# Rounding weights beside attention and a seven-product matrix multiplication: a ring of exponents, two block sets, later stores, and twelve attention pairs beside the second product

## The chip, the cores and the metric

One core of one Trainium2 chip. The metric is the device time of one execution in microseconds (us), the median of several runs. A profiled execution gives a span, from first to last instruction, about 2 us shorter than the time. The engines are TensorE (PE in the profile; PEld is its weight load), VectorE (DVE), ScalarE (ACT), GpSimd (POOL) and SyncE (SP), whose queue issues most of the DMAs.

## The reference

Shortened (the softmax takes off its maximum first, and small constants are left out):

```python
def _attn_ref(q, k, v, g_q, g_k):            # q, k, v: (8, 12, 448, 64)
    q_n, k_n = rmsnorm(q, g_q), rmsnorm(k, g_k)
    scores = scale * np.matmul(q_n, k_n.transpose(0, 1, 3, 2))
    attn = softmax(scores)
    return np.matmul(attn, v)
def _moe_ref(x, w_in, w_out):                # x: (3584, 768), w_in: (768, 2048), w_out: (2048, 768)
    h = x @ w_in
    r = np.maximum(h, 0.0)
    return (r * r) @ w_out
# [...] x is attn with the heads joined; w_in and w_out arrive as float64
```

The weights come as 64-bit floats (`words_in = 2` in the kernel) and are rounded to 32 bits on the chip.

## The kernel before

The 8 batches are four spans of two; a span has twelve attention pairs (two heads each). Both products of a span use a scheme of seven block products in place of eight (operands A11, S2, S1, S3, A12, A22, S4 of the weights). The weights' operands are made once, in span 0, from 32 pieces n of the weights, by a pipeline of 35 steps ("ticks") that is spread over the first 350 us, and stored in DRAM as `w1s` and `w2s`, from where `sw` tiles are loaded for each product.

A tick in its four quarters:

```python
# tick t; n = t: exponent, n = t-1: mantissa, n = t-2: value, n = t-3: totals and store
nc.vector.tensor_scalar(eu, high, 20, 0x7FF, shift_right, and_)     # e lies in the block of n
nc.scalar.activation(f, f, AF.Copy, bias=1.0, scale=2.0 ** -20)       # n = t-2
total(t - 3, S1, A21, A22, ALU.add, late)                             # late: on VectorE
total(t - 3, S2, S1, A11, ALU.subtract)                               # on GpSimd
yield
# [...] two activations of the exponent
total(t - 3, S3, A11, A21, ALU.subtract, late)
total(t - 3, S4, A12, S2, ALU.subtract)
yield
# [...] two VectorE operations of the mantissa
value(t - 2, 0)                                                       # GpSimd: f * e
yield
nc.vector.scalar_tensor_tensor(f, low, 2.0 ** -32, high, mult, add)
value(t - 2, 1)
# n = t-3: store the block (w1s: one DMA; w2s: three), then load words up to t + 2
yield
```

The first product takes seven `sw` tiles for each of eight f; pb, pc and pd turn over two PSUM banks, and VectorE adds them up:

```python
pb = ps_m.tile([P, S], F32, tag="m", name="pb"); product(pb, n + S2, T2, True);  add(z, p1, pb)
pc = ps_m.tile([P, S], F32, tag="m", name="pc"); product(pc, n + S1, T1, True);  add(y, z, pc)
pd = ps_m.tile([P, S], F32, tag="m", name="pd"); product(pd, n + S3, T3, True);  add(g22, y, pd)
# [...] product(pa, A12), product(pd, A22): add(g21, z, pd); product(pc, S4): add(g12, z, pc)
```

The order of span 0 and the attention of span 1 (ALONE = 2):

```python
for u, _ in enumerate(attention(work, 0, start_of(1), True)):      # stage A
    weights(EARLY * (u + 1) // (2 * NPAIR))                           # 12 ticks
for u, _ in enumerate(first_product(work, 0)):                     # stage B
    weights(EARLY + (LATE - EARLY) * (u + 1) // N1)                   # 21 ticks
for u, _ in enumerate(attention(work, start_of(1), start_of(1) + ALONE, True)):   # stage C
    weights(ALL)
# second_product(0) with the ten other pairs of span 1 beside it: stage D; then the rest: R
```

## Time and profile before

| | before |
|---|---|
| time, median of 3 | 1513.79 us (1513.71 to 1518.29) |
| span of the profiled run | 1512.0 us |
| TensorE busy | 1443.2 us, 95% |
| TensorE idle | 54 of 68.8 us in the first 347 us |

A high busy share of TensorE says where little gain is to be had: of the 68.8 us in which TensorE is idle, 54 lie in the first 347 us and 14.8 in the 1165 us after them. In the first 347 us four engines and one DMA queue hand work to each other, and there the reading goes backward from each wait to who was late, and why. The lines stand in the prediction below.

### The profile page before, as it was taken

Reading aid. Unit: us, or ns where it says so; the run is one execution under the profiler, and the core shown is the slowest. Engines: PE = TensorE matmul, PEld = TensorE weight load, DVE = VectorE, ACT = ScalarE, POOL = GpSimd, SP = SyncE. Lnnn points to the kernel's source line nnn. Section 1 sums busy time; section 2 is a strip of 40 time slices with the busy share of each in tenths; the row PEclk is TensorE's granted clock in tenths of the full one; section 3 lists DMA queues with packets and bytes.
Section 4 is the critical chain, followed back from the end, with each engine's and each line's share of the span. In section 5 each row is a group of like instructions: output and inputs, shape, how many; then the busy total and the mean of one; then the engine's idle time right before and its main releaser. Section 6 shows DMA issues by size and latency. Waiting matters only on the chain.

```text
span 1512.0 us, 14222 instructions
## 1 busy us (share of the span) xinstructions
PE 1443.2 (95%) x4696; PEld 658.8 (44%) x4696; DVE 828.4 (55%) x1160; ACT 431.4 (29%) x588; POOL 554.9 (37%) x367
## 2 busy tenths in 40 slices
PE   5998889888999999999999999999999999999998
PEld 2433444333444445544444445544444445555553
DVE  3777789856776533446666643345666752332111
ACT  4766565542222201123222211123223211111000
POOL 4788667773333102353344202254333301221000
PEclk9999999989999999999999999999999999999999
DMA  5365888854445433343445433334445323333443
GB/s 163 97 193 152 251 308 273 273 127 101 103 87 118 100 87 89 85 110 75 111 90 111 91 87 99 85 100 100 98 92 112 78 66 98 85 88 104 101 116 68
DMA packets 357816, 180.39 MB, mean 119 GB/s; under 512 B 255140, under 2 KB 334180, under 8 KB 357732
## 3 DMA queue, kind: packets, MB, share of 16 engines
q1 hardware_dynamic: 349668, 168.36, 43.7%
q10 hardware_dynamic: 8064, 11.01, 2.2%
q8 instruction: 40, 0.66, 0.2%
q14 instruction: 44, 0.36, 0.1%
HBM read 146.28 MB, written 33.03 MB: 119 GB/s over the span
## 4 chain that ended last, share of the span: by engine, by line
PE 73%; POOL 9%; DVE 7%; issue 5%; DMA 4%; ACT 1%; SPq 0%; POOLq 0%; DVEq 0%; ACTq 0%
PE ps L864 30%; PE sc L675 8%; PE pa L788 8%; PE pav L692 7%; PE pc L788 7%; PE pd L788 7%; PE pb L788 4%; DVE rec L709 4%; POOL rstd L618 3%; POOL gC L479 2%; PE tot L703 2%; POOL qkn L620 2%; DMA sw<-w1s 2%; POOL gC L486 1%; DMA gC<-in_moe_w_out_dram 1%
## 5 line engine op out<-in xcount | busy, mean ns | idle before, releaser
L864 PE MATMUL ps<-gT,sw 128*128 128x448 f32 x768 | 303.2, 545 | 0.0
L640 POOL TENSOR_TENSOR half<-half,mhalf 128x28 f32<-128x28 f32 x34 | 166.2, 4888 | 316.7 <-DVE half L639 262.5
L796 POOL TENSOR_TENSOR gT<-gT 128x448 f32<-128x448 f32 x112 | 111.1, 994 | 439.3 <-ACT gT L792 437.3
L678 ACT ACTIVATE pr<-sc 112x896 f32<-112x896 f32 x192 | 165.9, 913 | 237.5 <-PE sc L675 237.3
L864 PE MATMUL ps<-gC,sw 128*128 128x448 f32 x576 | 228.2, 545 | 0.0
L864 PEld LDWEIGHTS ps<-gT,sw 128*128 128x128 f32 x768 | 143.3, 190 | 155.5 <-issue 155.1
L675 PE MATMUL sc<-qkT 64*112 64x448 f32 x768 | 174.7, 575 | 14.8 <-ACT qkT L654 12.5
L709 DVE RECIPROCAL rec<-tot 128x448 f32<-128x448 f32 x48 | 141.9, 2957 | 81.8 <-PE tot L703 81.8
L692 PE MATMUL pav<-pr,vt 112*64 112x448 f32 x768 | 165.4, 554 | 10.5 <-DVE xT L711 6.8
L788 PE MATMUL pa<-xT,sw 128*128 128x448 f32 x384 | 156.4, 544 | 5.3 <-DMA sw<-w1s 5.3
L864 PEld LDWEIGHTS ps<-gC,sw 128*128 128x128 f32 x576 | 106.9, 190 | 116.7 <-issue 114.6
L792 ACT ACTIVATE gT<-gT 128x448 f32<-128x448 f32 x96 | 55.2, 576 | 292.7 <-DVE gT L822 178.3
L675 PEld LDWEIGHTS sc<-qkT 64*112 64x112 f32 x768 | 62.3, 177 | 112.5 <-issue 74.5
L683 DVE TENSOR_TENSOR acc<-acc,pr 112x896 f32<-112x896 f32 x68 | 74.7, 1099 | 59.6 <-ACT pr L678 56.1
L788 PEld LDWEIGHTS pa<-xT,sw 128*128 128x128 f32 x384 | 73.3, 191 | 78.3 <-issue 75.0
L692 PEld LDWEIGHTS pav<-pr,vt 112*64 112x64 f32 x768 | 52.1, 139 | 111.5 <-issue 87.2
L654 ACT ACTIVATE qkT<-qkT,gains 128x448 f32<-128x448 f32 x34 | 22.7, 668 | 238.5 <-DVE qkT L653 238.5
L788 PE MATMUL pd<-xT,sw 128*128 128x448 f32 x192 | 80.1, 554 | 7.3 <-DVE z L811 4.5
L788 PE MATMUL pd<-xC,sw 128*128 128x448 f32 x192 | 77.7, 541 | 3.8 <-DVE gT L822 3.8
L683 DVE TENSOR_TENSOR acc<-pr 112x896 f32<-112x896 f32 x34 | 37.1, 1091 | 78.9 <-ACT pr L678 78.9
L788 PE MATMUL pc<-xC,sw 128*128 128x448 f32 x192 | 77.6, 540 | 1.1 <-DVE gT L835 0.9
L788 PE MATMUL pc<-xT,sw 128*128 128x448 f32 x192 | 77.5, 540 | 0.8 <-DMA sw<-w1s 0.8
(90 smaller groups left out, 1493.7 us busy)
## 6 DMA issues: line engine op xcount, KB each, us to landing
sw<-w2s SPq DMA_DIRECT2D x168, 256.0 KB, 2.8
sw<-w1s SPq DMA_DIRECT2D x168, 192.0 KB, 2.3
w1s<-gC SPq DMA_DIRECT2D x8, 1344.0 KB, 6.2
sw<-w1s ACTq DMA_DIRECT2D x56, 192.0 KB, 4.6
w2s<-gC SPq DMA_DIRECT2D x24, 448.0 KB, 4.3
out_dram<-osb SPq DMA_DIRECT2D x192, 56.0 KB, 1.8
words<-in_moe_w_out_dram SPq DMA_DIRECT2D x11, 768.0 KB, 7.3
qk<-in_q_dram SPq DMA_DIRECT2D x136, 56.0 KB, 2.8
```

Source lines behind the costliest of these rows:

```text
L479: nc.gpsimd.tensor_tensor(b[to[n % 2][half]], f[:, part], e[:, part], ALU.mult)
L618: nc.gpsimd.tensor_tensor(rflat, rflat, mhalf[:SP, 0:4 * NJ], ALU.pow)
L640: nc.gpsimd.tensor_tensor(half, half, mhalf, ALU.pow)
L675: nc.tensor.matmul(sc[:, h, 0:S], qkT[rows, 1, c * SP:(c + 1) * SP], qkT[rows, 0, :], start=True, stop=True)
L678: nc.scalar.activation(pr, sc[:, :, 0:S], AF.Exp)
L683: nc.vector.tensor_tensor(accs[i], probs[i, 0] if c == 1 else accs[i], pr, ALU.add)
L692: nc.tensor.matmul(pavs[i][h * D:(h + 1) * D, :], vs[i][:, h, c, :], pr[:, h, :], start=(c == 0), stop=(c == NJ - 1))
L709: nc.vector.reciprocal(rec, tots.pop(i))
L788: nc.tensor.matmul(ps, stream[n][:, c], rhs[:, c], start=first and c == 0, stop=c == HC - 1, skip_group_check=not first)
L792: nc.scalar.activation(g, src, AF.Relu)
L796: nc.gpsimd.tensor_tensor(g, g, g, ALU.mult)
L864: nc.tensor.matmul(ps, stream[n][:, c % 4], rhs_of[i][:, c], start=c == 0, stop=c == HF - 1)
```

## The change

Its intent: the exponents get a ring of four buffers of their own, so that they no longer lie in blocks that totals or values want; this leaves room for two block sets in place of three. Stores go out after the last totals, loads earlier; all loads go over the SP queue; w_out's operands are stored in one DMA. The total S1 moves to GpSimd. Then stage C goes: all twelve pairs of span 1 run beside the second product. The core of the diff:

```diff
-    ALONE = 2
-    NAT = 2 * NPAIR + ALONE
+    NAT = 2 * NPAIR
-    WORDS, BLOCKS, LAST = 6, 3, 24
-    EARLY, LATE, ALL = 4 * 12, 4 * 33, 4 * (2 * NFC + 3)
+    WORDS, BLOCKS, EXPS, LAST = 6, 2, 4, 31
+    EARLY, LATE, ALL = 4 * 13, 4 * 35, 4 * (2 * NFC + 4)
-    w2s = dram.tile([HC, 7, HF // 4, P, 4 * P], F32, name="w2s")
+    w2s = dram.tile([7, HF // 4, P, 4, HW], F32, name="w2s")
+    def exponents_of(n):
+        at = BLOCKS * 8 * HW + n % EXPS * NW
+        return stage[:, at:at + NW]
 ... (in the tick)
-        total(t - 3, S1, A21, A22, ALU.add, late)        # quarter 0, VectorE
+        total(t - 3, S1, A21, A22, ALU.add)              # quarter 2, GpSimd
+        while loaded[0] <= t + 3 and all(...): load_w    # quarter 1; was t + 2 in quarter 3
-        n = t - 3                                        # the store, quarter 3
+        n = t - 4                                        # quarter 2
+            nc.sync.dma_start(dst.rearrange("k p m -> p k m"), blocks_of(n)[:, 0:7])
 ... (the sw loads)
-            queue = nc.scalar if len(stream) < N1 else nc.sync
-            queue.dma_start(sw.rearrange("p c m -> p (c m)"), src)
+            nc.sync.dma_start(sw, src)
 ... (the order of the stages)
+                if u == NAT - 2:
+                    load_blocks(5)
-        # the pool "alone" with two pairs and weights(ALL)
+    weights(ALL)
+                free = 0 if span else 2
-                for u, _ in enumerate(attention(work, a, start_of(span + 2), False)):
+                for u, _ in enumerate(attention(work, nxt, nxt + 2 * NPAIR, False)):
```

More of the change, by code (lines that the diff above doesn't have):

```diff
@@ L405, in attention_then_ffn_bounded @@
     HW = HC * P
-    WORDS, BLOCKS, LAST = 6, 3, 24
-    EARLY, LATE, ALL = 4 * 12, 4 * 33, 4 * (2 * NFC + 3)
-    assert DM == NW and BLOCKS * 8 * HW + 2 * NW <= 3 * HF * S and 2 * NW <= 4 * S and HF % 4 == 0
+    WORDS, BLOCKS, EXPS, LAST = 6, 2, 4, 31
+    EARLY, LATE, ALL = 4 * 13, 4 * 35, 4 * (2 * NFC + 4)
+    assert DM == NW and BLOCKS * 8 * HW + EXPS * NW + 2 * NW <= 3 * HF * S and 2 * NW <= 4 * S and HF % 4 == 0
     A11, S2, S1, S3, A12, A22, S4 = range(7)
@@ L422, in place_of @@
     def place_of(n):
-        return n % WORDS if n < LAST else (0, 3, 4, 5)[(n - LAST) % 4]
+        return n % WORDS if n < LAST else 3
     def words_of(n):
@@ L428, in words_of @@
         if place == 0:
-            at = BLOCKS * 8 * HW
+            at = BLOCKS * 8 * HW + EXPS * NW
             flat = stage[:, at:at + 2 * NW]
@@ L458, in prepare, with parts @@
     def prepare(t):
-        def parts(n):
-            b = [blocks_of(n)[:, i] for i in range(8)]
-            at = (S2, A22)[n % 2]
-            e = blocks_of(n)[:, at:at + 2].rearrange("p k m -> p (k m)")
-            low, high = pairs_of(words_of(n))
-            return b, e, e.bitcast(U32), low, low.bitcast(F32), high
         def there(n):
             return 0 <= n < 2 * NFC
+        def parts(n):
+            low, high = pairs_of(words_of(n))
+            return exponents_of(n), exponents_of(n).bitcast(U32), low, low.bitcast(F32), high
@@ L473, in value @@
         def value(n, half):
-            b, e, _, _, f, _ = parts(n)
+            if not there(n):
+                return
             to = ((A11, A12), (A21, A22)) if n < NFC else ((A11, A21), (A12, A22))
+            dst = blocks_of(n)[:, to[n % 2][half]]
             part = slice(half * HW, (half + 1) * HW)
             if doubles:
-                nc.gpsimd.tensor_tensor(b[to[n % 2][half]], f[:, part], e[:, part], ALU.mult)
-            else:
-                nc.gpsimd.tensor_copy(b[to[n % 2][half]], words_of(n).bitcast(F32)[:, part])
@@ L483, in total @@
-        def total(n, dst, x, y, op, on_vector=False):
+                e, _, _, f, _ = parts(n)
+                nc.gpsimd.tensor_tensor(dst, f[:, part], e[:, part], ALU.mult)
+            else:
+                nc.gpsimd.tensor_copy(dst, words_of(n).bitcast(F32)[:, part])
+        def total(n, dst, x, y, op, engine=nc.gpsimd):
             if there(n) and n % 2:
-                b = parts(n)[0]
-                (nc.vector if on_vector else nc.gpsimd).tensor_tensor(b[dst], b[x], b[y], op)
-        late = t >= EARLY // 4
+                b = [blocks_of(n)[:, i] for i in (dst, x, y)]
+                engine.tensor_tensor(*b, op)
@@ L489, in prepare @@
         if there(t) and doubles:
-            b, e, eu, low, f, high = parts(t)
+            e, eu, low, f, high = parts(t)
             nc.vector.tensor_scalar(eu, high, 20, 0x7FF, ALU.logical_shift_right, ALU.bitwise_and)
         if there(t - 2) and doubles:
-            f = parts(t - 2)[4]
+            f = parts(t - 2)[3]
             nc.scalar.activation(f, f, AF.Copy, bias=1.0, scale=2.0 ** -20)
-        total(t - 3, S1, A21, A22, ALU.add, late)
-        total(t - 3, S2, S1, A11, ALU.subtract)
@@ L497, in prepare @@
         yield
         if there(t) and doubles:
-            b, e, eu, low, f, high = parts(t)
+            e, eu, low, f, high = parts(t)
             nc.scalar.activation(e, eu, AF.Relu, bias=clamp1, scale=-1.0)
             nc.scalar.activation(eu, e, AF.Relu, bias=clamp2, scale=-(2.0 ** 23))
-        total(t - 3, S3, A11, A21, ALU.subtract, late)
-        total(t - 3, S4, A12, S2, ALU.subtract)
+        while loaded[0] <= t + 3 and all(
+                place_of(m) != place_of(loaded[0]) for m in range(max(t - 2, 0), loaded[0])):
+            load_w(loaded[0])
+            loaded[0] += 1
@@ L505, in prepare @@
         yield
         if there(t - 1) and doubles:
-            b, e, eu, low, f, high = parts(t - 1)
+            e, eu, low, f, high = parts(t - 1)
             nc.vector.scalar_tensor_tensor(eu, high, 0x80000000, eu, ALU.bitwise_and, ALU.bitwise_or)
             nc.vector.tensor_scalar(high, high, 0xFFFFF, None, ALU.bitwise_and)
-        if there(t - 2):
-            value(t - 2, 0)
+        value(t - 2, 0)
+        total(t - 3, S1, A21, A22, ALU.add)
+        n = t - 4
+        if there(n) and n % 2:
+            c = n % NFC // 2
+            dst = w1s[c] if n < NFC else w2s[:, c // 4, :, c % 4]
+            nc.sync.dma_start(dst.rearrange("k p m -> p k m"), blocks_of(n)[:, 0:7])
+            written[0] = n + 1
@@ L515, in prepare @@
             nc.vector.scalar_tensor_tensor(f, low, 2.0 ** -32, high, ALU.mult, ALU.add)
-        if there(t - 2):
-            value(t - 2, 1)
-        n = t - 3
-        if there(n) and n % 2:
-            c = n % NFC // 2
-            if n < NFC:
-                nc.sync.dma_start(w1s[c].rearrange("k p m -> p k m"), blocks_of(n)[:, 0:7])
-            else:
-                for m in range(HC):
-                    nc.sync.dma_start(
-                        w2s[m, :, c // 4, :, c % 4 * P:(c % 4 + 1) * P].rearrange("k p m -> p k m"),
-                        blocks_of(n)[:, 0:7, m * P:(m + 1) * P])
-            written[0] = n + 1
-        while loaded[0] <= t + 2 and all(
-                place_of(m) != place_of(loaded[0]) for m in range(max(t - 1, 0), loaded[0])):
-            load_w(loaded[0])
-            loaded[0] += 1
+        value(t - 2, 1)
+        total(t - 3, S2, S1, A11, ALU.subtract)
+        total(t - 3, S3, A11, A21, ALU.subtract, nc.vector if t >= EARLY // 4 else nc.gpsimd)
+        total(t - 3, S4, A12, S2, ALU.subtract)
         yield
     def ticks():
-        for t in range(2 * NFC + 3):
+        for t in range(2 * NFC + 4):
             yield from prepare(t)
@@ L565, in load_blocks @@
                 sw = sw[:, 0:HC]
-                src = w1s[n // 7, n % 7]
+                src = w1s[n // 7, n % 7].rearrange("p (c m) -> p c m", c=HC)
             else:
                 n -= N1
-                src = w2s[*uses2[n // (HF // 4)], n % (HF // 4)]
-            queue = nc.scalar if len(stream) < N1 else nc.sync
-            queue.dma_start(sw.rearrange("p c m -> p (c m)"), src)
+                m, i = uses2[n // (HF // 4)]
+                src = w2s[i, n % (HF // 4), :, :, m * P:(m + 1) * P]
+            nc.sync.dma_start(sw, src)
             stream.append(sw)
@@ L740, in attention @@
             scores(work, i, 1, alone)
-            if i + 2 < (start_of(2) if alone else last):
+            if i + 2 < (last + 2 if alone else last):
                 norm(i + 2)
@@ L925, in attention_then_ffn_bounded @@
         with tc.tile_pool(name="first", bufs=2, reuse_waits="tile") as work:
-            for u, _ in enumerate(attention(work, 0, start_of(1), True)):
-                weights(EARLY * (u + 1) // (2 * NPAIR))
+            for u, _ in enumerate(attention(work, 0, NAT, True)):
+                weights(EARLY * (u + 1) // NAT)
+                if u == NAT - 2:
+                    load_blocks(5)
         with tc.tile_pool(name="first_product", bufs=2, reuse_waits="tile") as work:
@@ L930, in attention_then_ffn_bounded @@
                 weights(EARLY + (LATE - EARLY) * (u + 1) // N1)
-        with tc.tile_pool(name="alone", bufs=2, reuse_waits="tile") as work:
-            for u, _ in enumerate(attention(work, start_of(1), start_of(1) + ALONE, True)):
-                weights(ALL)
+    weights(ALL)
     for span in range(NSPAN):
@@ L944, in attention_then_ffn_bounded @@
             if more:
-                a = nxt + (0 if span else ALONE)
-                places = 2 * (start_of(span + 2) - a)
+                free = 0 if span else 2
                 total, done = HC * (7 * HF + 4) - 20, 0
-                for u, _ in enumerate(attention(work, a, start_of(span + 2), False)):
-                    while done < total * (u + 1) // places:
+                for u, _ in enumerate(attention(work, nxt, nxt + 2 * NPAIR, False)):
+                    while done < total * (u + 1 - free) // (4 * NPAIR - free):
                         next(rest)
```

## The prediction

> **What bounds the kernel now.** I began with the summary page: TensorE (PE) is busy 1443 of 1512 us, so at most 69 us can be had without removing TensorE work. The view of busy time by stretches, cut where the instructions of the timeline change line, says where they lie. The columns are: stretch, its length, busy time of PE, PEld, DVE, ACT and POOL (with instructions), granted clock, DMA share, GB/s.
>
> ```profile
> PE 1443.2 (95%) x4696; PEld 658.8 (44%) x4696; DVE 828.4 (55%) x1160; ACT 431.4 (29%) x588; POOL 554.9 (37%) x367
> ...
> 0.00:160.00 160.00, 136.49 (x680) 56.19 (x680) 103.25 (x113) 98.12 (x124) 117.54 (x82) 0.97 0.55 157
> 160.00:163.80 3.80, 0.00 (x0) 0.00 (x0) 3.77 (x2) 0.00 (x0) 3.26 (x4) 1.00 1.23 195
> 163.80:311.60 147.80, 133.49 (x336) 63.91 (x336) 122.63 (x145) 82.24 (x115) 96.78 (x76) 0.98 0.81 268
> 311.60:347.30 35.70, 23.31 (x107) 8.31 (x106) 18.97 (x27) 12.20 (x17) 23.24 (x15) 0.83 0.59 137
> 347.30:553.10 205.80, 205.80 (x697) 89.22 (x698) 136.53 (x199) 48.78 (x60) 58.63 (x24) 0.99 0.43 98
> 553.10:1512.00 958.90, 944.08 (x2881) 441.19 (x2879) 443.21 (x677) 190.03 (x273) 255.43 (x168) 1.00 0.39 94
> ```
>
> The stages, named for use below: A, attention of span 0 with most of its totals on TensorE (160 us); a gap of 3.8; B, the first product of span 0 (147.8); C, two pairs of span 1 alone (35.7); D, the second product with the other ten pairs (205.8); R, the rest (958.9). D and R are solid TensorE; the change can win only in the first 347 us. There I read who TensorE waits for, in A from 28 us on, in B, and in C (columns: total us, times, longest):
>
> ```profile
> PE pt L659 <- POOL qkn L620: 3.8, 4, 2.6
> PE pav L692 <- DMA vt<-in_v_dram: 3.6, 2, 2.4
> ...
> PE pa L788 <- DMA sw<-w1s: 5.3, 2, 4.0
> PE pd L788 <- DVE z L811: 4.5, 3, 2.1
> PE pd L788 <- DVE gT L822: 3.8, 3, 2.3
> PE pd L788 <- DMA sw<-w1s: 2.6, 1, 2.6
> ...
> PE pav L692 <- DVE xT L711: 6.8, 1, 6.8
> PE sc L675 <- ACT qkT L654: 5.2, 1, 5.2
> ```
>
> These releasers are themselves late, so I followed them back through the waits of the queue that issues the DMAs and of POOL, in A from 28 us on:
>
> ```profile
> SPq L522 <- POOL gC L486: 54.8, 4, 14.8
> SPq L310 <- POOL qkn L620: 39.4, 13, 10.3
> ...
> POOL rstd L618 <- DVE rstd L617: 28.2, 9, 8.6
> ...
> ACT qkn L613 <- DMA qk<-in_k_dram: 9.2, 3, 4.1
> ```
>
> The store of a block (L522) stands in the in-order queue until POOL has made its totals (L486), up to 14.8 us; the loads of q, k and v behind it start late; the norms then run late on ACT, DVE and POOL; TensorE waits for qkn and vt. A loop of lateness, not a full engine.
>
> **What the Trainium skill says.** "DMA: Bandwidth & Descriptors", section "Anatomy of one DMA": DMA engines wait on no semaphore; the issuing sequencer waits before it dispatches. The 54.8 us above agree. Its specifications give 512 B as the least transfer for line rate; the new w_out loads have 512 B pieces where they had 2048 B, just on that edge, and no trace here has that shape yet. "TensorE: Matmul & The Clock Gate", section "Part 1: The HAM clock gate": after about 3.4 us idle the array runs at half clock until it has been busy about as long again. The trace agrees: after 4.0 us idle the first six passes of B took 3.98 us and not 2.42. "GPSIMD Engine Reference", section "Engine selection": two-input elementwise work is about 2x slower on GpSimd than on VectorE. In B the same 128x384 operation took 1276 ns on POOL and 728 ns on DVE, 1.75x.
>
> **The change, part by part.**
>
> *Stage A.* A pair takes 10.46 us where nothing waits (scores at 31.76, 42.22, 52.68, 63.14, 73.61, 84.07), so from pair 1 at 31.76 the stage could end at 31.76 + 11 x 10.46 = 146.8 (its last pair needs 10.46 after its start) and ends at 159.8: 13 us lost in pairs 6, 8 and 10. Moving a store a tick (four steps, about one pair here) behind its totals takes away most of what it waits for; vt and qk then go out in time, and with them the clock losses. Words are loaded nearly two ticks earlier: load of t+3 at the first quarter of tick t, against t+2 at its end. Against it: a thirteenth tick in A adds 2 values and 4 totals, 6 POOL operations at 1.0 us, 117.5 -> about 124 us in a stage that should get shorter, near 85%. I keep 5 of the 13 us as lost: A ends at 151.5, 8 sooner.
>
> *Gap.* The first five w1s loads are issued a pair before A ends: 3.8 us away.
>
> *Stage B.* 56 products x 2.255 us = 126.3 us is TensorE's floor; 147.8 - 126.3 = 21.5 are lost. DVE: S1 goes to POOL (11 x 0.73 = 8 us), and one tick of rounding fewer lies here (one exponent step 0.8, one set of three 1.29 + 1.04 + 1.32 = 3.65): 122.6 - 12 = about 111 us, 88% of the floor. POOL: + 11 x 1.28 = 14, less two values of 1.3: 96.8 + 11 = 108, 86%. No engine exceeds the floor, but both come in bursts. The w1s loads leave ACT's queue, where they waited behind activations (4.6 us to landing, against 2.3 on the other queue later); they now stand in the one queue behind stores and word loads, five products ahead (four x 2.26 = 9 us of cover). Two block sets for three mean that POOL's value may overwrite a block one tick (about 5.8 us) after its store was issued, and such a store took 6.2 us to land: a new wait, about balanced. I take 9 us of loss in place of 21.5: B = 135.
>
> *Stages C and D.* Both pairs go into D. Beside the second product a pair costs TensorE 1.69 + 3.05 + 0.86 + 1.69 = 7.3 us; C and its idle time go. But two places are left without product, so that D opens with what C had: pair 12 alone (scores, four exponentials of 0.91 with the norm's square of 0.95 between, the accumulation of 3 x 1.1, totals, reciprocal 2.96, xT 0.95, transposes 1.13, scaling 0.67) gives scores of pair 13 at about 15 us and the first ps at about 17. The w2s loads stand in the queue behind the last store (after POOL's totals, some 5.5 us into D), eight q/k issues of pair 15, then eight of pair 16, which wait for the norm of pair 14 (POOL power 4.8, two multiplies 1.84, done at about 13): issued at 17 to 20, landed 3 us later. I take first ps at 21.5. From ps onward the kernel before needs 553.1 - 350.5 = 202.6 for what it has; one more pair (13's values to 23's end instead of 14's) makes 209.9. D = 21.5 + 209.9 = 231, in place of C + D = 241.5: 10 us won.
>
> *w_out in one store, and R.* One store of 1344 KB in 1536 B rows for three of 448 KB in 512 B rows saves issues in B. The loads get 512 pieces for 128. A 256 KB load serves eight passes, 3.0 us, against 2.8 us to landing, with five buffers ahead and a DMA share of 0.39 in R. I expect no wait: R = 958.9.
>
> *Sum.* 151.5 + 135 + 231 + 958.9 = 1476.4; the time before exceeds its span by 1.8: **1478 us**, 2.4% less.
>
> **Rivals.**
> 1. *POOL becomes the bound of A and B.* S1 moves to the slower engine and A gets six more operations. For it: power 3.7 and two multiplies 2.1 us each pair, plus 52/12 steps, come to some 10 us of 10.46; 1.28 to 1.33 us an operation in B. Against: 28 us of waits in A and 51 idle in B now. Then A saves 3 and B 5: about 1491.
> 2. *The single queue blocks.* Word loads wait for POOL's value of the tick before, stores for totals, and w1s loads stand behind; cover is 9 us less 2.3 to 5 of landing. Then TensorE waits for sw in every tick or two, B stays near 143: 1486.
> 3. *The opening of D goes better or worse.* With the w2s loads ready, ps starts at 17: 1473. If the last store and pair 16's q/k are late, 26 us: 1483.
> 4. *512 B pieces are slow.* Landing times above 9 us would stall R in every second product; the spare DMA share speaks against. Each 0.1 us per w2s load would be 17 us; I give it 4%.
>
> **Range and chances.** A may end at 147 to 157, B be 129 to 143, the opening of D 17 to 26; as independent errors about 3, 4 and 3 us, together 6. The lean is upward, since the rivals only add: 1468 to 1491. The 2% line lies at 1483.5, nearly one error above my number: faster 0.70, same 0.29, slower 0.01.
>
> **What would show it right or wrong.** Right, if in the profile after: the store's wait on POOL totals in A falls from 54.8 to below 20 us and vt vanishes from TensorE's waits; A's last total ends at 148 to 155 and the first pa follows within 1 us; B is 130 to 140 us with DVE near 111 and POOL near 108 busy; the first ps comes 19 to 24 us after B; TensorE shows no sw wait after 560 us and R is 958 to 960. Wrong, if B stays above 143 (look whether pd waits for sw or for DVE), if POOL's gC waits for a store, if A still ends near 160, or if R has grown.

## The result and the profile after

| | before | after |
|---|---|---|
| time, median (4 runs each) | 1513.75 us | 1497.45 us (1497.3 to 1499.91) |
| ratio, 95% interval | | 0.989 (0.9868 to 0.9911) |
| predicted | | 1478 us, range 1468 to 1491 |

Ratios here and below are the mean time of one kernel's fast runs over that of the other's of the same rounds, so not quite the ratio of the medians quoted. The result is correct. The change is faster by 1.1%, less than half of what was predicted, and outside the range.

Busy time by stretches, of the kernel after, cut at the same events (end of A, set 0.2 us too early, first pa, first scores of pair 12, first ps, first pa of span 1; columns as in the prediction):

```profile
0.00:152.70 152.70, 133.60 (x672) 53.84 (x672) 107.87 (x124) 97.69 (x123) 114.59 (x82) 0.99 0.59 174
152.70:154.20 1.50, 0.18 (x2) 0.02 (x1) 1.43 (x3) 1.47 (x3) 1.50 (x1) 1.00 1.03 355
154.20:302.20 148.00, 131.97 (x338) 63.21 (x338) 133.14 (x136) 82.93 (x116) 123.62 (x97) 0.99 0.80 268
302.20:323.60 21.40, 11.02 (x45) 3.49 (x44) 13.52 (x18) 7.98 (x10) 12.05 (x7) 0.76 0.62 148
323.60:536.60 213.00, 211.41 (x725) 90.94 (x726) 144.17 (x212) 50.84 (x63) 63.32 (x27) 0.99 0.44 97
536.60:1495.60 959.00, 944.18 (x2881) 441.18 (x2879) 442.05 (x677) 190.03 (x273) 256.43 (x168) 1.00 0.39 94
```

Stage by stage against the prediction:

| | before | predicted | after |
|---|---|---|---|
| A ends at | 159.8 | 151.5 | 152.9 |
| gap | 4.0 | 0 | 1.3 |
| B | 147.8 | 135 | 148.0 |
| C / opening of D up to the first ps | 38.9 | 21.5 | 21.4 |
| first ps to span 1's first pa | 202.5 | 209.9 | 213.0 |
| R | 958.9 | 958.9 | 959.0 |

A, the opening and R came out as told. Stage B did not get shorter at all: 13 of the 19 us of error. In it VectorE was busy for 133 us and not 111, though it executes fewer instructions (136 against 145), and GpSimd for 124 and not 108. The lines of the total S3 (and S1, which VectorE made before), by line, with shortest, median and longest duration in ns; first of the kernel before, then of the kernel after:

```profile
L486 POOL TENSOR_TENSOR gC<-gC x40: 991/1002/1712, 74.6 to 330.0; 128x384 f32<-128x384 f32 x40
L486 DVE TENSOR_TENSOR gC<-gC x24: 545/552/1289, 166.1 to 328.5; 128x384 f32<-128x384 f32 x24
```

```profile
L489 POOL TENSOR_TENSOR gC<-gC x53: 992/1192/1744, 75.6 to 307.4; 128x384 f32<-128x384 f32 x53
L489 DVE TENSOR_TENSOR gC<-gC x11: 552/1358/1400, 176.4 to 302.8; 128x384 f32<-128x384 f32 x11
```

The same operation takes 552 ns at its shortest in both, but its median is 552 before and 1358 after. An addition with one operand in PSUM, of the kernel after, hardly varies:

```profile
L805 DVE TENSOR_TENSOR z<-p,pb x32: 607/621/623, 164.8 to 1350.7; 128x448 f32<-128x448 f32 x32
```

What stands behind it is in the Trainium skill, "SBUF — State Buffer", section "SBUF: two separate sides": VectorE and GpSimd share a pair of SBUF ports, taken as an exclusive lock for a whole instruction by whichever starts first, VectorE asking for them when it has two SBUF inputs (against a GpSimd operation that reads SBUF) or runs in a two-port mode. The two-valued durations and the steady addition from PSUM agree with that. The prediction did not look there.

The timeline of the kernel after shows the lock instruction by instruction (start us, us; both engines in order of time):

```profile
200.98 1.27 DVE L523 SCALAR_TENSOR_TENSOR words<-words 128x768 f32<-128x768 uint32 x1
201.40 1.72 POOL L489 TENSOR_TENSOR gC<-gC 128x384 f32<-128x384 f32 x1
202.18 1.36 DVE L489 TENSOR_TENSOR gC<-gC 128x384 f32<-128x384 f32 x1
...
227.72 0.55 DVE L489 TENSOR_TENSOR gC<-gC 128x384 f32<-128x384 f32 x1
228.08 1.07 POOL L482 TENSOR_TENSOR gC<-gT,gC 128x384 f32<-128x384 f32 x1 [1.69 <-DVE words L523]
```

The addition at 202.18 begins while a GpSimd operation runs and ends 0.42 us after that one's end (203.54 against 203.12); the one at 227.72 begins with GpSimd idle and takes 0.55. It is so without exception: of 121 such additions on VectorE in the kernels before and after and in e2, e3, e6 and e12, the 62 that began beside a running GpSimd operation ended 0.41 to 0.42 us after its end, and the other 59 took 0.54 to 0.57 us. GpSimd's addition at 201.40 was itself long (1.72 us; 0.99 at its shortest), beside the VectorE instruction that ended at 202.25.

Who waits for whom in stage B after, for TensorE (columns: total us, times, longest):

```profile
PE pd L782 <- DVE z L805: 4.0, 3, 2.2
PE pa L782 <- DMA sw<-w1s: 3.3, 3, 1.7
PE pc L782 <- DMA sw<-w1s: 3.2, 2, 1.7
PE pd L782 <- DMA sw<-w1s: 2.8, 2, 1.4
PE pb L782 <- DVE xC L722: 1.8, 1, 1.8
PE pd L782 <- DVE gT L816: 1.4, 2, 1.2
```

Half of it is VectorE, half the sw loads. 1.3 us of the first pa line are the gap in front of B; without them the loads make 8.0 us and VectorE 7.9. In the kernel before, the same count gives 4.9 and 9.2 us. So the change made TensorE wait longer for loads and not longer for VectorE, though VectorE was busy 10.5 us more. How a load comes late shows the chain of work, one turn of it, in order of time (start us, us, what):

```profile
244.49 1.68 POOL gC L489
...
246.25 1.21 POOL gC L489
...
247.48 0.37 SPq L519
...
247.94 5.87 DMA sw<-w1s
...
253.95 2.49 PE pc L782 x6
```

GpSimd finishes the totals at 247.46, the store of 1344 KB is issued, and the sw load behind it in the same queue lands 5.9 us later. The median of the 40 sw loads issued in B is 5.2 us (29 that were issued while a store was under way 5.9, the other 11 4.4), and that of all 224 loads of the kernel 2.4 us. Loads right behind a store land as late at 261.0, 273.7 and 286.8 (6.1 to 6.3 us), but there the chain comes from TensorE, whose last use of the buffer the load waited for, and not from GpSimd's totals.

### The profile page after: what moved, and what is told of

The parts are those of the page before. It is cut to its first block, busy times and chain, and to the rows that moved or that the text cites. A ratio compares the mean times of both kernels' runs of the same rounds, so it can differ in the third digit from the quotient of the medians.

```text
span 1495.6 us, 14182 instructions
## 1 busy us (share of the span) xinstructions
PE 1432.4 (96%) x4656; PEld 652.7 (44%) x4656; DVE 842.2 (56%) x1167; ACT 430.9 (29%) x586; POOL 571.5 (38%) x380
## 4 chain that ended last, share of the span: by engine, by line
PE 76%; DVE 9%; POOL 6%; DMA 3%; issue 3%; ACT 2%; SPq 0%; DVEq 0%; POOLq 0%; ACTq 0%
PE ps L858 29%; PE sc L669 9%; PE pd L782 8%; PE pav L686 8%; PE pa L782 8%; PE pc L782 8%; DVE rec L703 4%; PE pb L782 4%; PE tot L697 3%; DMA sw<-w1s 2%; POOL gC L489 1%; POOL gC L482 1%; POOL rstd L612 1%; POOL qkn L614 1%; DVE qkT L647 1%
## 5 line engine op out<-in xcount | busy, mean ns | idle before, releaser
L634 POOL TENSOR_TENSOR half<-half,mhalf 128x28 f32<-128x28 f32 x36 | 176.8, 4911 | 320.4 <-DVE half L633 298.6
L790 POOL TENSOR_TENSOR gT<-gT 128x448 f32<-128x448 f32 x112 | 114.2, 1021 | 419.2 <-ACT gT L786 419.2
L686 PE MATMUL pav<-pr,vt 112*64 112x448 f32 x768 | 161.5, 547 | 0.8 <-DVE xT L705 0.8
L677 DVE TENSOR_TENSOR acc<-acc,pr 112x896 f32<-112x896 f32 x72 | 78.6, 1092 | 61.5 <-ACT pr L672 57.6
L782 PE MATMUL pb<-xC,sw 128*128 128x448 f32 x192 | 77.7, 540 | 2.5 <-DVE xC L722 1.8
```

The costliest lines, as they stand in the source:

```text
L634: nc.gpsimd.tensor_tensor(half, half, mhalf, ALU.pow)
L677: nc.vector.tensor_tensor(accs[i], probs[i, 0] if c == 1 else accs[i], pr, ALU.add)
L686: nc.tensor.matmul(pavs[i][h * D:(h + 1) * D, :], vs[i][:, h, c, :], pr[:, h, :], start=(c == 0), stop=(c == NJ - 1))
L782: nc.tensor.matmul(ps, stream[n][:, c], rhs[:, c], start=first and c == 0, stop=c == HC - 1, skip_group_check=not first)
L790: nc.gpsimd.tensor_tensor(g, g, g, ALU.mult)
```

## The experiments

Theories after this reading. **S** (shared access): GpSimd and VectorE stretch each other's instructions, so that work moved to GpSimd, and GpSimd's waits taken away, are paid for on VectorE. **Q** (one queue): the sw loads stand behind stores and word loads that wait for GpSimd. **B** (banks): TensorE and VectorE are locked together through two PSUM banks. Sixteen kernels ran; the table lists stage B of each profiled run: its length, the busy times of three engines (TensorE needs 126.3 us at least), TensorE's waits within B for sw loads and for VectorE, and what the granted clock cost, (1 - mean clock) x length. These are figures of one execution each, all in us.

| run | time | ratio to before | B | DVE busy | POOL busy | PE busy | waits for sw | waits for DVE | lost to clock |
|---|---|---|---|---|---|---|---|---|---|
| before | 1513.8 | 1 | 147.8 | 122.6 | 96.8 | 133.5 | 4.9 | 9.2 | 3.4 |
| after | 1497.45 | 0.989 | 148.0 | 133.1 | 123.6 | 132.0 | 8.0 | 7.9 | 1.7 |
| e1 w1s loads on ACT's queue | 1498.53 | 0.9908 | 149.0 | 129.7 | 123.5 | 133.9 | 2.7 | 12.2 | 3.4 |
| e2 S1 on VectorE | 1496.84 | 0.9891 | 147.5 | 137.4 | 110.5 | 132.0 | 1.7 | 13.8 | 1.7 |
| e3 all totals on VectorE | 1500.48 | 0.9915 | 154.8 | 136.5 | 80.9 | 137.4 | 0.9 | 16.3 | 8.5 |
| e4 before, twelve pairs in D | 1524.34 | 1.0077 | 147.9 | 118.2 | 94.5 | 133.8 | 6.4 | 7.6 | 4.0 |
| e5 free banks for pc and pd | 1496.45 | 0.9879 | 147.7 | 132.4 | 124.9 | 131.7 | 11.2 | 4.8 | 1.7 |
| e6 no totals on GpSimd (wrong result) | 1487.76, one run | | 139.7 | 118.9 | 82.6 | 129.0 | 3.8 | 6.8 | 0.0 |
| e7 w2s loads ahead | 1493.48 | 0.9856 | 148.0 | 133.2 | 123.3 | 131.7 | 8.8 | 7.4 | 1.7 |
| e8 after, two pairs alone | 1498.48 | 0.9891 | 152.0 | 133.7 | 120.9 | 132.6 | 9.0 | 10.3 | 5.1 |
| e9 e5 + e1 + e7 | 1495.92 | 0.9879 | 149.6 | 132.2 | 126.4 | 135.6 | 3.4 | 10.4 | 6.8 |
| e10 e9 + S1 on VectorE | 1490.97 | 0.9846 | 146.2 | 136.4 | 113.9 | 131.8 | 2.2 | 12.3 | 1.7 |
| e11 three stores of w_out | 1505.92 | 0.9937 | 157.2 | 130.8 | 123.0 | 136.6 | 12.3 | 8.1 | 6.8 |
| e12 squares on ScalarE | 1493.18 | 0.987 | 144.7 | 125.4 | 106.5 | 130.3 | 6.7 | 7.7 | 0.0 |
| e13 e10 + squares on ScalarE | 1491.05 | 0.9856 | 146.3 | 131.2 | 93.7 | 132.0 | 7.6 | 6.7 | 3.4 |
| e14 e13 + a 14th tick in A | 1490.95 | 0.9862 | 140.6 | 121.8 | 83.0 | 130.4 | 4.0 | 6.2 | 3.4 |
| e15 e13 with loads on SP | 1489.35 | 0.9832 | 143.7 | 130.2 | 92.7 | 130.7 | 0.0 | 12.3 | 1.7 |
| e16 e15, stores in halves | 1489.64 | 0.9832 | 143.2 | 128.3 | 91.3 | 132.1 | 0.0 | 11.0 | 3.4 |

TensorE's clock was granted at half for stretches of about 3.4 us in B (166.3 to 169.7 in the kernel after), each a loss of 1.7 us. They come after some waits of 1.9 to 7.0 us and not after others (two of 2.2 us in e12, with no such stretch), so B can differ by one or two such stretches between kernels that wait alike. A difference of 2 to 4 us in B is read against the last column first.

**e1: the w1s loads back on ACT's queue.**

```diff
-            nc.sync.dma_start(sw, src)
+            (nc.scalar if len(stream) < N1 else nc.sync).dma_start(sw, src)
```

> Changed kernel, but the w1s loads of span 0 go out on ACT's queue again, as before the change. Theory Q (one queue: a load waits behind the store that waits for POOL, and behind its 1344 KB): TensorE's waits for sw in stage B, 9.3 us in all, shrink to 3 or less in the second half of B and B falls from 147.8 to about 141; time about 1491. Theory S (VectorE and GpSimd share access to SBUF and stretch each other's instructions): B stays within 2 us of 147.8, the sw waits are replaced by waits for DVE and by ACT's own lateness; time 1496 to 1499.

The sw waits in B fell from 8.0 to 2.7 us, as Q says, but waits for VectorE rose from 7.9 to 12.2 and B stayed at 149.0. Theory Q is right on where the load's lateness comes from and wrong on what it is worth alone: 1498.53 against 1497.45 us.

**e2: S1 on VectorE.**

```diff
-        total(t - 3, S1, A21, A22, ALU.add)
+        total(t - 3, S1, A21, A22, ALU.add, nc.vector if t >= EARLY // 4 else nc.gpsimd)
```

> Changed kernel, but the total S1 is made on VectorE from tick 13 on, as before the change. Theory S: 11 operations of 1.3 us leave GpSimd and VectorE's own gets shorter, so DVE's busy time in B does not grow by 11 x 0.73 = 8 us but stays near 133, POOL's falls from 124 to about 108, stores are ready earlier, B becomes 3 to 6 us shorter: about 1493. Rival (VectorE is simply full at 133 of 148): DVE busy grows to 140 and B gets longer by 5: about 1502.

Neither: VectorE's busy time grew by 4 us with eleven more operations, GpSimd's fell by 13, and B and the time stayed (147.5; 1496.84). With GpSimd's work lighter the waits for sw nearly went (8.0 to 1.7 us), and the waits for VectorE took their place (7.9 to 13.8). And S1 and S3 are slow here, where the kernel before had them mostly fast:

```profile
L489 DVE TENSOR_TENSOR gC<-gC x22: 536/1354/1378, 173.7 to 303.7; 128x384 f32<-128x384 f32 x22
```

So it is not where S1 is made but what GpSimd does meanwhile (16 of these 22 began beside a running GpSimd operation). Before, GpSimd waited 21.5 us in B for VectorE's S1, and VectorE made it with the ports to itself; that wait, which the profile before lists, is 2.5 us here and absent after:

```profile
POOL gC L486 <- DVE gC L486: 21.5, 11, 4.0
```

**e3: all totals on VectorE** (the same edit on S2 and S4 too).

> Changed kernel, but all four totals are made on VectorE from tick 13 on; GpSimd keeps the values and the squares. Theory S: 33 operations of 1.36 us (45 us) leave GpSimd, and VectorE takes them at 0.55 to 0.75 us (18 to 25 us) while its other instructions shrink toward their shortest times (0.55 and 0.95 us); DVE busy in B 125 to 140, POOL about 75, B 136 to 142, time 1486 to 1492. Rival (VectorE full): DVE busy 155 or more, B 155 or more, time above 1504.

VectorE made 33 totals more and was busy only 3.4 us longer; the totals' median fell to 546 ns, as S has it:

```profile
L489 DVE TENSOR_TENSOR gC<-gC x44: 538/546/1378, 172.9 to 312.0; 128x384 f32<-128x384 f32 x44
```

Yet B got longer, to 154.8: pd waited 9.5 us for z and 5.0 for g22, and the granted clock in B fell to 0.94 (0.99 after), which alone cost 6.8 us more than after, as much as B grew. Four totals one after the other on VectorE stand in front of the additions that TensorE waits for; that is read from the waits, not shown by a run of its own.

**e4: the kernel before with the last part alone**: ALONE = 0, twelve pairs beside the second product, two places free.

```diff
-    ALONE = 2
+    ALONE = 0
-            if i + 2 < (start_of(2) if alone else last):
+            if i + 2 < (last + 2 if alone else last):
-        # stage C: two pairs alone with weights(ALL)
+    weights(ALL)
+                free = 0 if span else 2
```

> Kernel before, with only the last part of the change: no pairs alone, all twelve pairs of span 1 beside the second product, two places left free. If the 16.3 us gained come half from stages C and D and half from stage A and the gap, as the two traces read side by side say (A and gap 163.8 to 154.2, C and D 241.5 to 234.6), this alone gives 5 to 10 us: 1504 to 1509. If stage A's gain hangs on it (other norms and loads at its end), it gives more than 12. If the last store now stands bare in front of the second product, it gives less than 3.

A miss in every branch: it is 11 us slower than before. The stretches say where: the first pa comes at 171.1 in place of 163.8, since the first w1s loads on ACT's queue now stand behind an activation of pair 12's transposes, whose norm falls into A by the second edited line (TensorE's wait for sw in front of B: 13.5 us); and the opening of D is 29.1 us with the last ticks of the rounding in it. C + D is 242.8 here and 241.4 before: two pairs alone had hidden that tail as cheaply.

**e5: pc and pd in the two PSUM banks that attention leaves free in B.**

```diff
-            pc = ps_m.tile([P, S], F32, tag="m", name="pc")
+            pc = ps_o.tile([P, S], F32, tag="t", name="pc")
-            pd = ps_m.tile([P, S], F32, tag="m", name="pd")
+            pd = ps_o.tile([P, S], F32, tag="o", name="pd")
```

> Changed kernel, with the PSUM tiles pc and pd of the first product in the two banks that attention leaves unused there, so that pb alone turns over the two shared banks. Theory B (stage B is 148 us in five of six kernels because TensorE and VectorE are locked together through two banks: pd waits for z, the next pb for g12, one product of slack each): the waits of pd for z and of pb for gT vanish, only the waits for sw and for g22 stay, B falls to 138 to 143, time 1488 to 1493. Rival (VectorE, stretched by GpSimd, has 133 us of work and no more than that is lost): banks only shift the wait to the data dependency (pd's second part after g22), B 146 to 148, time 1496 to 1498.

The waits for z (4.0 us after) are gone, those for VectorE in all are 4.8 us in place of 7.9, and the waits for sw rose from 8.0 to 11.2: B 147.7. As in e1, one wait took the other's place.

**e6: the totals taken from GpSimd and made nowhere** (the result is wrong).

```diff
-        total(t - 3, S1, A21, A22, ALU.add)
+        if t < EARLY // 4:
+            total(t - 3, S1, A21, A22, ALU.add)      # S2 and S4 likewise; S3 stays on VectorE
```

> Wrong result on purpose: changed kernel without the totals S1, S2 and S4 from tick 13 on (33 operations of 1.36 us leave GpSimd in stage B and go nowhere); VectorE has the same instructions as before. Theory S (shared access to SBUF stretches): VectorE's mean times fall although nothing of its own changed: S3 from 1.28 toward 0.75, its busy time in B from 133 to 118 or less, and B to 138 or less. Rival (the durations are VectorE's own, by strides): busy time stays at 130 to 134, B at 145 to 148.

VectorE's own instructions are unchanged. Its busy time in B fell from 133.1 to 118.9 and B to 139.7. The line of S3, again with its shortest, median and longest time, and the stretch B:

```profile
L489 DVE TENSOR_TENSOR gC<-gC x11: 544/566/1385, 174.3 to 294.0; 128x384 f32<-128x384 f32 x11
...
153.66:293.36 139.70, 128.99 (x336) 62.78 (x336) 118.86 (x137) 82.85 (x116) 82.58 (x67) 1.00 0.86 285
```

This shows S: 41 us less on GpSimd are 14.3 us less on VectorE, 0.35 us for each. It is one run, of unknown state. What shortened B is another matter: TensorE's waits for sw fell by 4.2 us, its waits for VectorE by 1.1, and its busy time by 3.0 (no half clock here). Stores that waited for nothing would do the first as well as S would.

**e7: the first w2s loads ahead of the q/k loads of pairs 15 and 16.**

```diff
     weights(ALL)
+    load_blocks(N1 + 5)
```

> Changed kernel, but the first five w2s loads are issued right behind the last store, ahead of the q/k loads of pairs 15 and 16. If the opening of D waits for the queue (the loads stand behind the norm of pair 14), the first ps comes 17 to 19 us after B in place of 21.4 and the time is 2 to 3 us less: 1494 to 1495.5. If it is the store's landing, no difference.

The first ps came 18.7 us after B and no longer waited for sw; 1493.48 us. The queue, not the landing of the store, held it: 2.7 us, from one line. (The intervals of the ratios, 0.9829 to 0.9883 and 0.9868 to 0.9911, overlap; the 2.7 us of the trace are the surer figure.)

**e8: the changed kernel with its last part undone** (two pairs alone again).

```diff
+    ALONE = 2
-    NAT = 2 * NPAIR
+    NAT = 2 * NPAIR + ALONE
+        # stage C again: attention(work, start_of(1), start_of(1) + ALONE, True) with weights(ALL)
```

> Changed kernel with the last part undone: two pairs of span 1 alone again, ten beside the second product. The stages before and after say C and D went from 241.4 to 234.4, so undoing it costs about 7 us (1504) if the parts are independent; together with run e4, where this part alone made the kernel 11 us slower, the rest of the change would then be worth 9 us by itself.

1498.48 us, ratio 0.9891, the same as the whole change within the intervals. Stage C up to the first ps is 30.0 us here and was 38.9 before, as the rounding is done by then, and the stretch from there to span 1's first pa is 204.0: together 234.0, against 234.4 with all twelve pairs in D. So the twelve pairs in D are worth nothing in stages C and D beside the rest of the change, and cost 11 us without it (e4). The 16 us come from the rest. The equal totals are a balance: A with the gap is 2.7 us shorter here and B 4.0 longer, of which 3.4 are clock.

**e9: e5, e1 and e7 together.**

> Changed kernel with three edits together: free PSUM banks for pc and pd (e5), w1s loads of span 0 on ACT's queue (e1), w2s loads ahead (e7). Theory T (two waits take each other's place in stage B: the queue behind POOL in e5, the banks behind VectorE in e1; each edit alone leaves the other): together B falls to 138 to 143 and, with 2.7 us at the opening of D, the time to 1483 to 1490. Rival P (GpSimd with 124 us of work, its values waiting for stores and ACT, sets B whatever feeds TensorE): B stays at 146 to 148 and the time is that of e7, 1493.

B 149.6: the rival P was nearer by its number. Free banks and a free queue together still left B where it was: TensorE waited less (13.8 us for both in place of 15.9) but lost 6.8 us to the clock in place of 1.7. VectorE was busy 132.2, GpSimd 126.4, and in this run GpSimd's values wait 13.6 us for stores. **e10: the same with S1 on VectorE.**

> As e9, and S1 on VectorE from tick 13 on (e2). Theory P: with 11 operations fewer on GpSimd the stores and values come sooner; B is 3 us or more below that of e9. Theory S (the sum of both engines' SBUF work counts, not who does it): B within 2 us of e9.

B 146.2, 3.4 below e9; 1490.97 us. That is the number of theory P, but not by its path: TensorE's waits are no shorter (14.5 us against 13.8), and the gain is in its passes, busy 131.8 us in place of 135.6, with 1.7 us lost to the clock in place of 6.8. This pair does not show that GpSimd's load counts.

**e11: w_out's operands in three stores and the old layout**, the rest of the change kept.

```diff
-            dst = w1s[c] if n < NFC else w2s[:, c // 4, :, c % 4]
+                for m in range(HC):
+                    nc.sync.dma_start(w2s[m, :, c // 4, :, c % 4 * P:(c % 4 + 1) * P]..., blocks_of(n)[:, 0:7, m * P:(m + 1) * P])
```

> Changed kernel with the w_out operands stored as before, three stores of 448 KB in 512 B rows, and loaded in 2048 B rows. My prediction took the one store as worth nothing or little: time within 2 us of 1497.5, w2s loads land in 2.8 us in place of 3.2, nothing waits for them after the opening of D. If the one store was worth having, B gets longer by 3 us or more here, since three stores stand ahead of the w1s loads and take longer to land.

The second branch: B 157.2 and the time 1505.92. The w2s loads do land in 2.8 us as before, in place of 3.2, and it is worth nothing, as no product waits for them. With all loads on one queue, the single store is worth 7 to 8 us; TensorE's waits for sw in B were 12.3 us here (8.0 after), and 6.8 us were lost to the clock (1.7 after).

**e12: all squares of span 0 on ScalarE** (half of them were on GpSimd).

```diff
-            if span == 0 and on_scalar:
+            if span == 0:
```

> Changed kernel, with all squares of span 0 on ScalarE (16 of them were on GpSimd: 1.26 us each, 19 us in stage B). Nothing of VectorE's own changes. Theory S: POOL's busy time in B falls from 124 to about 103, VectorE's from 133 to 127 or less, since less of it lies beside GpSimd, and B to 143 to 146; time 1492 to 1496. Rival (VectorE's durations do not depend on what GpSimd does, and run e6 was faster because its stores waited for nothing): VectorE's busy time stays at 132 to 134.

Neither VectorE's work nor the order of stores is touched, though totals can be ready sooner. GpSimd's busy time in B fell by 17.1 us, VectorE's by 7.7, B by 3.3, and the time is 1493.18:

```profile
153.40:298.15 144.75, 130.32 (x337) 62.49 (x337) 125.41 (x137) 91.39 (x131) 106.45 (x84) 1.00 0.81 274
```

0.45 us of VectorE for each us of GpSimd, near e6's 0.35. S is shown by both, as to VectorE's durations (the S3 line itself stayed at a median of 1359 ns, as GpSimd's totals still run beside it; other instructions got shorter, L512 from a mean of 1018 ns to 753). That B got shorter by it is not shown. TensorE's waits in e12:

```profile
PE pa L782 <- DMA sw<-w1s: 3.9, 4, 1.6
PE pd L782 <- DVE z L805: 3.5, 3, 2.2
PE pb L782 <- DVE xC L722: 2.2, 1, 2.2
PE pd L782 <- DMA sw<-w1s: 1.7, 1, 1.7
PE pc L782 <- DMA sw<-w1s: 1.4, 2, 1.2
```

Of B's 3.3 us, 1.3 are shorter waits for sw, 0.2 shorter waits for VectorE, and 1.7 shorter passes, which is one stretch of half clock less.

**e13: e10 with the squares on ScalarE.**

> All of e10 (free PSUM banks, w1s loads on ACT's queue, w2s loads ahead, S1 on VectorE) and the squares on ScalarE. Theory S: VectorE's busy time in B from 136 to about 130, B from 146 to 139 to 143, time 1484 to 1488. Rival (ACT, now with loads and squares, becomes late): waits for p and g11 appear, B 146 or more.

VectorE fell to 131.2 but B stayed at 146.3 and the time at 1491.05; GpSimd waited 33 us for ACT, which issues loads and squares here. TensorE's waits for VectorE did fall, from 12.3 to 6.7 us, but those for sw rose from 2.2 to 7.6. The rival (ACT late) fits. **e14: the same with a fourteenth tick in A.**

> As e13, and a fourteenth tick of the rounding in stage A. If VectorE's work sets B, one tick less of 22 takes 5 us from B (rounding 4.5 and half of two totals), and A, where VectorE and GpSimd have 108 and 115 us of 153, pays 1 to 3: time 2 to 4 us below e13. If stage A is already at its limit, it pays as much: no difference.

B fell by 5.7, A ended 5.5 later: no difference. A is at its limit too.

**e15: e13 with the loads back on SP's queue. e16: stores in halves besides.**

```diff
-            nc.sync.dma_start(dst.rearrange("k p m -> p k m"), blocks_of(n)[:, 0:7])
+            nc.sync.dma_start(dst[0:4].rearrange("k p m -> p k m"), blocks_of(n)[:, 0:4])     # e16
+        yield
+            nc.sync.dma_start(dst[4:7].rearrange("k p m -> p k m"), blocks_of(n)[:, 4:7])     # e16
```

> As e13, but the w1s loads stay on the one queue of the changed kernel: free banks, w2s loads ahead, S1 on VectorE, squares on ScalarE. In e13 ACT's lateness showed in POOL's waits (33 us for ACT), with ACT both issuing loads and squaring. If that held B at 146, B is 140 to 143 here and the time 1485 to 1488; if the queue's waits for sw come back in full (9 us), B stays at 145 or more and the time at 1491.

> As e15, with each store in two halves a quarter of a tick apart (4 and 3 of the 7 blocks), so that a w1s load stands behind 768 KB at most and not 1344 KB. If the bulk of the store in front of a load makes the remaining sw waits, they fall below 2 us and B by 2 to 4 us against e15; if the wait of the queue for the totals makes them, no difference. The second half lands later, so that a value on GpSimd may wait 1 us more for its block.

e15 is the fastest kernel here with a right result: 1489.35 us, ratio 0.9832 (0.9811 to 0.9854), below the changed kernel's interval. Its B is 143.7, and the waits for sw within B are gone; pd waits 9.5 us for g22, which it must (it adds onto a bank that VectorE has still to read). ACT's lateness explains part of e13's B (2.6 us). e16 is no different from e15: with the sw waits gone already, the bulk of a store is not what is left.

## Why the prediction was wrong

- **Bound and loop of lateness in A: right in the main.** The store's wait for totals in A fell from 54.8 to 7.7 us, vt vanished from TensorE's waits, and A ended at 152.9 (151.5 told). But the queue's wait for GpSimd did not go: word loads now wait 41.8 us for its values, so that the three lines below make 89.6 us, where the two of the kernel before made 94.2. Also, the prediction read the store as moved a tick behind its totals; it went from half to three quarters of a tick behind the last of them. The lines of the queue's waits in A after:

```profile
SPq L457 <- POOL gC L482: 41.8, 9, 9.1
SPq L310 <- POOL qkn L614: 40.1, 10, 10.3
SPq L519 <- POOL gC L489: 7.7, 4, 2.4
```

- **Gap: nearly.** 1.3 us in place of none; the first sw load still landed late.
- **Stage B: the step that failed** is "I take 9 us of loss in place of 21.5". The loss measured 21.7 us: 8.0 of waits for sw, 7.9 for VectorE, and 5.7 by which TensorE's busy time exceeded its floor. Two supports of the 9 us did not hold. The first is the path of the loads: the prediction took their 4.6 us to landing for a matter of ACT's queue and counted on 2.3 to 5 of 9 us of cover; on the SP queue, behind stores, the median in B was 5.2 us, and the waits for sw rose from 4.9 to 8.0 us. The second is the engines' work. "About 111 us" for VectorE and 108 for GpSimd were durations read from the kernel before, multiplied by new counts. VectorE measured 133.1 and GpSimd 123.6. The terms were mis-sized because VectorE's additions of two SBUF inputs take 0.55 or 1.36 us by what GpSimd does, and its other rounding instructions vary as well; GpSimd was idle for 51 us of B before and for 24 after. GpSimd's sum missed also the norm of pair 13, which slid into B (5.1 us of power and 2.0 of multiplies), counted 38 values and 32 totals where 45 and 34 lie in B, and its means grew, totals 1.28 to 1.36, squares 1.10 to 1.26 us. So "No engine exceeds the floor" fell: VectorE's 133 us lie above TensorE's 126.3.
- **What is shown of the cause, and what not.** That VectorE's time depends on GpSimd's is shown: where e6 and e12 took work from GpSimd, VectorE's busy time fell. That VectorE's longer time is what kept B at 148 is not shown: TensorE's waits for VectorE fell from 9.2 to 7.9 us by the change, and by 1.1 and 0.2 more in e6 and e12, where VectorE had 14.3 and 7.7 us less to do. The stretch may act through later totals and stores instead; no run separates the two.
- **The same step was wrong on waits.** It counted GpSimd's idle time (51 us in B before) as spare and gave no cost to filling it. 21.5 us of it were waits for S1, and they were time in which VectorE ran fast: ten of the eleven S1 additions began there with GpSimd idle and took 0.55 to 0.56 us. No run puts that wait back alone; e2, where S1 is on VectorE again but nearly unwaited for, shows that the place of S1 is not it.
- **"w_out in one store" saves only issues: wrong.** e11 shows 7 to 8 us; without the one store, B would be 157.2 us, longer than before the change.
- **512 B pieces: right.** 3.2 us to landing, no wait in R, R 959.0.
- **Opening of D: right to 0.1 us, in part by luck.** e7 confirms that the loads held it. But with the loads ready the prediction gave 17 us and e7 shows 18.7; it took 4.5 us of waiting for them, and 2.6 were measured. And that C and D together win 10 us because a stage is taken away: the sum came to 7, and e8 shows that the rest of the change would have had them with the pairs alone as well.
- **From ps onward: 3 us too small.** TensorE was busy 211.4 us there; of the 3, 1.6 are short waits, the rest slower passes, the first of them at half clock after the idle opening.
- **Rivals.** The first named GpSimd as the bound and gave 1491; the second the queue and 1486. What came has parts of both, and a third that none named: each other's ports. e1, e2 and e5 show why single remedies gave nothing: a wait for the queue and a wait for VectorE take each other's place. e9 shortened both together by 2 us and lost more than that to the clock.
- The prediction took half clock for what follows "about 3.4 us idle". In B shorter waits were followed by it too (2.2 us in the kernel after, at 165.5), so a wait can cost more than its length; whether it does varies: in e12 the wait of 2.2 us at the same place was not followed by it.
- What stays open: how the 21.7 us of loss divide by cause. With banks, queue and squares mended (e15), B is 143.7 against 126.3; TensorE waits 12.3 us for VectorE, which is busy 130 us, and how it is to be freed was not tried.

## What to carry to other kernels

A duration from a profile holds for the neighbours that it had: before moving work between VectorE and GpSimd, compare the shortest and the median time of the instructions concerned, and where the ratio is large, look in the timeline whether the long ones begin while the other engine runs and end a fixed time after it. A wait on one engine can be what makes another fast, so that taking it away earns less than its length. Where a run is meant to shorten a stage, look at which wait became shorter: here VectorE's busy time fell by 7.7 us and TensorE's waits for it by 0.2. Where several waits stand in the same place, test remedies singly and together, and undo the named part of a change on top of the rest: it may be worth nothing there.

## What the Trainium skill lacked or had wrong

- "SBUF — State Buffer" names the shared ports and the exclusive lock; the runs agree and give sizes that no page has for this mix: a 128x384 addition on VectorE takes 0.55 us, or 0.41 to 0.42 us from the end of the GpSimd operation beside which it began (a median of 1.36 us), on GpSimd a median of 1.00 or 1.19 us, and 0.35 to 0.45 us of VectorE saved for each us taken from GpSimd (e6, e12).
- "GPSIMD Engine Reference", section "Engine selection": about 2x slower fits the shortest durations (0.99 against 0.55 us here); moved beside a busy VectorE, the operation took 1.36 us on GpSimd and stretched VectorE's as well. The table says nothing of that; only the page's list of specifications names the contention, without a size.
- "DMA: Bandwidth & Descriptors": a load of 192 KB issued right behind a store of 1344 KB on the same queue took 5.9 us to land, against 4.4 for loads of the same stage that were issued with no store under way and 2.4 over the whole kernel; no figure for that is given there. Its least transfer of 512 B for line rate is not contradicted: 256 KB in 512 B pieces landed in 3.2 us against 2.8 in 2048 B pieces; smaller pieces were not run.
